# Low halves of the MLP weights on VectorE instead of GpSimd, and the first two PReLUs ahead of a decode step

## Chip, cores and metric

One core of a Trainium2 chip runs the whole kernel in one launch. The metric is device time in microseconds (us) of that core. The kernel before takes 828.43 us (median of three runs, 828.38 to 828.44). The profile is of one further execution, which took 827.54 us; the span that its records cover is 825.8 us, so 1.7 us lie around the span.

The engines are named as in the profile: PE is TensorE (PEld its weight loads), DVE is VectorE, ACT is ScalarE, POOL is GpSimd, SP is the engine that issues most of the transfers.

## What is computed

Three stages follow one another (the reference, cut):

```
attn = softmax(where(mask, q @ k.T / 8, -1e9)) @ v      # 4 x 8 heads, 576 positions, 64 wide
x    = attn as [2304, 512]
h    = x @ w_in                                          # 512 -> 2048, float64 weights
g    = max(h, 0) + alpha * min(h, 0)                     # PReLU, one alpha for each of 2048 columns
x    = g @ w_out                                         # 2048 -> 512, float64 weights
e    = argmax(x @ w_gate); out = gate * sigmoid * (relu(x @ w1[e]) @ w2[e])   # 8 experts
```

Heads 0 to 3 see a local window of 32 positions, heads 4 to 7 every 32nd position. The weights of the PReLU MLP arrive as float64 and are sent to the chip as pairs of 32-bit words.

## The kernel before

**Tiles.** The 2304 tokens are taken in six blocks of 384 (BLK). The 2048 columns of the MLP are taken in 16 chunks of 128 (NC1). For each block and each chunk there are twelve matmuls of the first product (lines 439 to 441: high times high, low times high, high times low, for four slices of the contraction), a PReLU, a split of the result into a rounded high half and a low half, and nine matmuls of the second product (lines 473 to 475).

**High and low halves.** An operand of these products is held as two tiles, the value rounded by the write to the matmul's own float type and the rest. For the weights this is done once, in the first block, by decode, chunk by chunk. One chunk is 128 partitions x 1024 values (512 of w_in, 512 of w_out). Its steps are:

- decode_a (line 402, ACT): the upper words, scaled, into a buffer called stage;
- decode_b (lines 406 and 407, DVE): a shift, and the top bits of the lower words merged in;
- decode_s (line 413, DVE): the sign merged in; after it the raw words are free;
- decode_c (line 421, ACT): the high half into the first 1024 columns of the weight tile w; and (line 422, POOL) the low half, stage minus high half, into the other 1024 columns. After line 422 the stage buffer is free. There are three such buffers.

**Order.** The order on each engine is the order in which the program issues the instructions, written out by hand. There are two parts that matter here.

The prologue is 13 attention steps (lines 1129 to 1145), in which chunk k begins its decoding at step 2 + 2k and does one step of it at each attention step, so that chunks 0 to 3 are decoded and chunk 4 has had decode_a, decode_b and decode_s when it ends. Line 1148 therefore issues nothing; line 1149 issues decode_a of chunk 5. Then, for n = 0 and 1, follow the last three matmuls of the first product, the PReLU (mlp_act) and the split (mlp_split).

The main loop (line 1170) runs over n, the pair of block and chunk. In iteration n of the first block the order is: exponentials and normalisation of one attention group, the first product of chunk n + 2, the values of an earlier group (line 328), their copy to xh on ACT (line 367) and the rest xl on DVE (line 372), the PReLU of chunk n + 2, decode_c of chunk n + 4, scores of a new group and their row maxima on DVE (line 252), decode_b and decode_s of chunk n + 5, a third of the second product of chunk n, transposes of an earlier group (line 313), the other two thirds, decode_a of chunk n + 6, and the split of chunk n + 2 (line 459 on ACT, line 460 on DVE).

Three couplings run across the engines. The first product of n + 2 writes one of two PSUM banks called h, which the split of n (line 460 last) frees. The values and the transposes share one PSUM bank T, so the transposes of an iteration wait until DVE has written xl of the same iteration (line 372). The normalisation is two small DVE instructions (lines 295 and 296) and one multiplication on POOL (line 297), which stands in POOL's queue together with line 422.

Of the kernel before, what the change touches and what calls it, by code (L numbers as in the profile page):

```python
# [7 lines left out]
F32 = mybir.dt.float32  # L8
# [3 lines left out]
AF = mybir.ActivationFunctionType  # L12
ALU = mybir.AluOpType
# [10 lines left out]
NC1 = FF // P  # L24
# [18 lines left out]
DEC = 4  # L43
# [40 lines left out]
def attention_prelu_mlp_routed_experts_kernel(  # L84
# [11 lines left out]
    nc = tc.nc  # L96
# [28 lines left out]
    with tc.manual_schedule():  # L125
# [251 lines left out]
        raw_t, w_t = {}, {}  # L377
# [6 lines left out]
        def w_tile(c, dt, name):  # L384
            return wpool.tile(
                [P, 2048], dt, tag="wa" if c < NA else "wb", name=name, bufs=NA if c < NA else NC1 - NA
            )

        def load_w(c):
            raw_t[c] = w_tile(c, I32, "raw64")  # L390
            nc.sync.dma_start(raw_t[c], wp[c].bitcast(I32))


        dec_t = {}
# [21 lines left out]
            raw_t.pop(c)  # L416

        def decode_c(c):
            t = dec_t.pop(c)
            w = w_t[c] = w_tile(c, F32R, "w")  # L420
            nc.scalar.activation(out=w[:, :1024], in_=t, func=AF.Copy)
            nc.gpsimd.tensor_tensor(out=w[:, 1024:], in0=t, in1=w[:, :1024].bitcast(F32), op=ALU.subtract)

        def w_in(c, part, k):
            return w_t[c][:, part * 1024 + k * P : part * 1024 + (k + 1) * P]
# [6 lines left out]
        def mlp_in(n, ks=range(KD)):  # L432
            blk, c = divmod(n, NC1)
            xh, xl = xt(blk)
            if n not in h_t:
                h_t[n] = bank("h", 2)
            ph = h_t[n]
            for k in ks:
                mm(ph[:, :BLK], w_in(c, 0, k), xh[:, k, :], start=(k == 0), stop=False)  # L439
                mm(ph[:, :BLK], w_in(c, 0, k), xl[:, k, :], start=False, stop=False)  # L440
                mm(ph[:, :BLK], w_in(c, 1, k), xh[:, k, :], start=False, stop=(k == KD - 1))  # L441

        def mlp_act(n):
            c = n % NC1
            ph = h_t.pop(n)
            v = ph[:, :BLK]
            a = xpool.tile([P, BLK], F32, tag="a", name="a", bufs=2)
            nc.scalar.activation(out=a, in_=v, func=AF.Relu)  # L448
            nc.scalar.activation(out=v, in_=v, func=AF.Relu, scale=-1.0)  # L449
            nc.vector.scalar_tensor_tensor(  # L450
                out=v, in0=v, scalar=nalpha[:, c : c + 1], in1=a, op0=ALU.mult, op1=ALU.add
            )
            h_t[n] = v

        def mlp_split(n):
            v = h_t.pop(n)
            gh = xpool.tile([P, BLK], F32R, tag="gh", name="gh", bufs=3)
            gl = xpool.tile([P, BLK], F32R, tag="gl", name="gl", bufs=2)
            nc.scalar.activation(out=gh, in_=v, func=AF.Copy)  # L459
            nc.vector.tensor_tensor(out=gl, in0=v, in1=gh.bitcast(F32), op=ALU.subtract)  # L460
            g_t[n] = (gh, gl)
# [606 lines left out]
        def load_ws(k):  # L1068
            for _, c in zip(range(k), loads):
                load_w(c)  # L1070
# [22 lines left out]
        def att_back(s):  # L1093
            if on(s - LV):
                att_rest(s - LV)
            for n in v_at.pop(s, ()):
                load_v(n)

        def att_step(s, tags, ttag, vtag):

            att_front(s)
            if on(s - 1):
                att_exp(s - 1)
            if on(s):
                att_scores(s, tags)
            if on(s - LV):
                att_values(s - LV, vtag)
                att_store(s - LV)
            if on(s - LT):
                att_transpose(s - LT, ttag)  # L1110
            if on(s):
                att_max(s)
            if on(s - 1):
                att_norm(s - 1)
            att_back(s)
# [4 lines left out]
        steps_done = {}  # L1120

        def decode(k, n):

            steps = [decode_a, decode_b, decode_s, decode_c]
            for f in steps[steps_done.get(k, 0) : n]:
                f(k)
            steps_done[k] = max(steps_done.get(k, 0), min(n, 4))

        for s in range(NPRO):
            att_step(s, ("h", "h") if s % 2 else ("S", "X"), "acc0" if s % 2 else "T", "acc1" if s % 2 else "acc2")  # L1130
# [4 lines left out]
            if s == 4:  # L1135
# [3 lines left out]
                    out=wg_hl[:, :, 2 * E :], in0=wg_sb, in1=wg_hl[:, :, : 2 * E].bitcast(F32), op=ALU.subtract  # L1139
                )  # L1140
                nc.vector.memset(acc_oh[:, 0, :], 0.0)
            for k in range(NC1):
                n = s - (T0[k] if k < len(T0) else 99)
                if n >= 0:
                    decode(k, n + 1)

        span[:] = [FIRST + EXTRA if EXTRA < LV else 0, NG]
        decode(DEC, 3)
        decode(DEC + 1, 1)
        for n in range(2):  # L1150
            mlp_in(n, range(KD - 1, KD))
            mlp_act(n)
            mlp_split(n)
        last = NBLK * NC1
        turn_at, logits_at = {}, {}
        for blk in range(NBLK - 1):
            for j in range(TPB):
                c = 2 * j + 1 if blk < NBLK - 2 else j
# [11 lines left out]
        for n in range(last):  # L1170
            blk, c = divmod(n, NC1)
            todo = []
            if blk + 1 < len(steps_of) and c < NC1 - 2:
                s0, s1 = steps_of[blk + 1]
                k = s1 - s0
                todo = list(range(s0 + k * c // (NC1 - 2), s0 + k * (c + 1) // (NC1 - 2)))
            for s in todo[:-1]:
                att_step(s, ("S", "X"), "T", "T")
            s = todo[-1] if todo else -9
            if on(s - 1):  # L1180
                att_exp(s - 1)
                att_norm(s - 1)
            if n + 2 < last:
                mlp_in(n + 2)
            if on(s - LV):
                att_values(s - LV, "T")
                att_store(s - LV)
            att_back(s)
            if n + 2 < last:
                mlp_act(n + 2)  # L1190
            if n + DEC < NC1:
                decode(n + DEC, 4)
            att_front(s)
            if on(s):
                att_scores(s, ("S", "X"))
                att_max(s)
            if n + DEC + 1 < NC1:
                decode(n + DEC + 1, 3)
            mlp_out(n, range(1))
            if on(s - LT):  # L1200
                att_transpose(s - LT, "T")
            mlp_out(n, range(1, 2))
            if (blk - 1, c) in logits_at:
                logits(blk - 1, logits_at[blk - 1, c])
            if (blk - 1, c) in turn_at:
                turn(blk - 1, turn_at[blk - 1, c])
            if blk > 0 and c == (7 if blk < NBLK - 1 else 4):
                gather_logits(blk - 1)
                rest = route_parts(blk - 1)
                next(rest)  # L1210
            if blk > 0 and c == (8 if blk < NBLK - 1 else 5):
                next(rest, None)
            if blk > 0 and c == (9 if blk < NBLK - 1 else 6):
                rank(blk - 1)
            mlp_out(n, range(2, TPB))
            load_ws(1)
            if n + DEC + 2 < NC1:
                decode(n + DEC + 2, 1)
            if n + 2 < last:
                mlp_split(n + 2)  # L1220
            if c == NC1 - 1 and blk == 3:
                s_a.close()
                epool = s_x.enter_context(tc.tile_pool(name="epool", bufs=1))
                idx_in = epool.tile([P, NSLOT], I32, name="idx_in")
                idx_out = epool.tile([P, NSLOT], I32, name="idx_out")
                idx_any = epool.tile([1, 1], I32, name="idx_any")
                e_i32 = epool.tile([1, NSLOT], I32, name="e_i32")
                taken = epool.tile([P, NTT], F32, name="taken")
                used = epool.tile([P, E], F32, name="used")
                nc.vector.memset(taken, 0.0)  # L1230
            if blk == NBLK - 1:
                if c == 6:
                    for _ in plan_parts(True):
                        pass
                    load_expert(0, 0)
                    load_expert(0, 1)
                if c == EL:
                    lists(True)
                    indices(True)
                if c in (9, 10, 11):  # L1240
                    gathers(0)
                if c == 11:
                    split_expert(0, 0)
                    load_expert(1, 0)
                if c == 13:
                    turn_x(0, 0)
                if c == 14:
                    turn_x(0, 1, bank("X"))
                    gathers(2)
                    split_expert(1, 0)  # L1250
                    load_expert(2, 0)
                if c == 15:
                    turn_x(1, 0)
            if c == NC1 - 1:
                evacuate(blk)
# [236 lines left out]
```

## Time and profile before

| | |
|---|---|
| median of three runs | 828.43 us |
| profiled execution / its span | 827.54 us / 825.8 us |
| PE busy | 783.3 us, 95% |
| DVE busy | 465.1 us, 56% |
| ACT busy | 427.6 us, 52% |
| POOL busy | 223.9 us, 27% |

These shares are means over stages with different limits. The page cuts the span into 40 slices of about 20.6 us; DVE reads 4979997345... in tenths, so its first 150 us are another stage than what follows. PE waits are listed by who ended them; an instruction that is itself held up while it runs shows as a long one, not as idle time, so durations of one line are compared with each other as well.

### The profile page before, as it was taken

The page shows a single profiled execution, that of the slowest core. Times are in us where ns is not written, and L with a number is a line of the kernel's source. Part 1 is how long each engine was busy: PE and PEld are TensorE (multiplying, and loading weights), DVE is VectorE, ACT ScalarE, POOL GpSimd, SP SyncE. Part 2 cuts the span into 40 slices and gives each one's busy share as a digit, 9 for nine tenths or more (in the row PEclk, how much of TensorE's full clock was granted, in tenths as well). Part 3 has the DMA queues.
Part 4 walks back from the last instruction along what each step waited for, and adds up shares of the span by engine and source line. Part 5 has one row for each costly group of instructions (what it writes and reads, how often), then busy time and mean ns, then how long its engine had stood idle before and what let it go on. Part 6 is the DMA issues. An engine that isn't in the chain of part 4 may idle for free. (4 is left out here: it accounts for less than half of the span.)

```text
span 825.8 us, 13693 instructions
## 1 busy us (share of the span) xinstructions
PE 783.3 (95%) x5035; PEld 659.0 (80%) x5035; DVE 465.1 (56%) x980; ACT 427.6 (52%) x1057; POOL 223.9 (27%) x152
## 2 busy tenths in 40 slices
PE   7778889999999999999999999999989998999996
PEld 4566767888888888888898898889879876878884
DVE  4979997345544454556333434657695447854422
ACT  6847676445544454555333333265534656655542
POOL 2734444011100011111000000113474465546422
PEclk9789899999999999999999999999999999999998
DMA  9707411111200121101000100553224577787421
GB/s 342 303 1 298 167 56 49 33 33 46 84 18 1 47 87 64 36 11 39 2 1 1 39 1 1 204 191 125 56 90 159 176 268 250 281 290 270 161 88 41
DMA packets 22621, 91.04 MB, mean 110 GB/s; under 512 B 3082, under 2 KB 7312, under 8 KB 15376
## 3 DMA queue, kind: packets, MB, share of 16 engines
q1 hardware_dynamic: 18816, 78.52, 26.8%
q0 software_dynamic: 3728, 11.55, 4.0%
q8 instruction: 41, 0.67, 0.3%
q14 instruction: 36, 0.29, 0.1%
HBM read 105.78 MB, written 9.97 MB: 140 GB/s over the span
## 5 line engine op out<-in xcount | busy, mean ns | idle before, releaser
L439 PE MATMUL h<-xh,w 128*128 128x384 f32 x384 | 131.2, 342 | 4.1 <-DVE gl L460 3.8
L440 PE MATMUL h<-xl,w 128*128 128x384 f32 x384 | 130.5, 340 | 0.7 <-DVE xl L372 0.7
L441 PE MATMUL h<-xh,w 128*128 128x384 f32 x384 | 130.4, 340 | 0.0
L450 DVE SCALAR_TENSOR_TENSOR h<-h,nalpha,a 128x384 f32<-128x384 f32 x96 | 59.9, 624 | 116.1 <-ACT h L449 116.0
L473 PE MATMUL acc<-w,gh 128*128 128x512 f32 x288 | 125.3, 435 | 0.0
L297 POOL TENSOR_TENSOR p<-p,sm 96x512 f32<-96x512 f32 (+2 forms) x47 | 48.2, 1026 | 283.6 <-DVE sm L296 260.5
L888 DVE TENSOR_TENSOR wx<-raw,wx 128x1024 fp32r<-128x1024 f32 x72 | 97.1, 1392 | 46.9 <-ACT wx L886 46.6
L475 PE MATMUL acc<-w,gl 128*128 128x512 f32 x288 | 114.3, 397 | 0.0
L474 PE MATMUL acc<-w,gh 128*128 128x512 f32 x288 | 114.1, 396 | 0.0
L448 ACT ACTIVATE a<-h 128x384 f32<-128x384 f32 x96 | 47.2, 491 | 105.9 <-PE h L441 105.9
L886 ACT ACTIVATE wx<-raw 128x1024 fp32r<-128x1024 f32 x96 | 94.6, 1056 | 7.6 <-DMA raw<-in_wexp_dram 7.6
L1042 PE MATMUL acc<-wx,hh 128*128 128x512 f32 x304 | 97.0, 401 | 0.0
L888 POOL TENSOR_TENSOR wx<-raw,wx 128x1024 fp32r<-128x1024 f32 x24 | 63.1, 2629 | 90.7 <-ACT wx L886 90.6
L439 PEld LDWEIGHTS h<-xh,w 128*128 128x128 f32 x384 | 73.4, 191 | 9.6 <-DVE gl L460 5.5
L440 PEld LDWEIGHTS h<-xl,w 128*128 128x128 f32 x384 | 73.2, 191 | 4.8 <-DVE xl L372 1.0
L441 PEld LDWEIGHTS h<-xh,w 128*128 128x128 f32 x384 | 73.2, 191 | 0.0
L460 DVE TENSOR_TENSOR gl<-h,gh 128x384 fp32r<-128x384 f32 x96 | 53.3, 555 | 33.0 <-PE acc L475 18.2
L895 POOL DMA_INDIRECT xg<-rows,idx_in x23 | 29.3, 1274 | 145.4 <-ACT h L449 139.0
L1042 PEld LDWEIGHTS acc<-wx,hh 128*128 128x128 f32 x304 | 56.6, 191 | 11.2
L475 PEld LDWEIGHTS acc<-w,gl 128*128 128x128 f32 x288 | 54.6, 190 | 13.2
L459 ACT ACTIVATE gh<-h 128x384 fp32r<-128x384 f32 x96 | 46.7, 486 | 34.8 <-DVE h L450 34.7
L473 PEld LDWEIGHTS acc<-w,gh 128*128 128x128 f32 x288 | 54.5, 189 | 10.6 <-issue 0.3
(259 smaller groups left out, 1548.3 us busy)
## 6 DMA issues: line engine op xcount, KB each, us to landing
raw<-in_wexp_dram SPq DMA_DIRECT2D x64, 1024.0 KB
raw<-in_wp_dram SPq DMA_DIRECT2D x16, 1024.0 KB
qk<-in_qkv_dram SPq DMA_DIRECT2D x10, 576.0 KB
rows<-stage SPq DMA_DIRECT2D x15, 256.5 KB
v<-in_qkv_dram SPq DMA_DIRECT2D x8, 320.0 KB
qk<-in_qkv_dram SPq DMA_DIRECT2D x4, 384.0 KB
v<-in_qkv_dram SPq DMA_DIRECT2D x6, 256.0 KB
qk<-in_qkv_dram SPq DMA_DIRECT2D x4, 224.0 KB
```

The source lines that it names most:

```text
L297: (nc.vector if gi in NRV else nc.gpsimd).tensor_tensor(out=pt[:r, :nu, :kk], in0=pt[:r, :nu, :kk], in1=sm[:r, :nu].unsqueeze(2).to_broadc ...
L439: mm(ph[:, :BLK], w_in(c, 0, k), xh[:, k, :], start=(k == 0), stop=False)
L440: mm(ph[:, :BLK], w_in(c, 0, k), xl[:, k, :], start=False, stop=False)
L441: mm(ph[:, :BLK], w_in(c, 1, k), xh[:, k, :], start=False, stop=(k == KD - 1))
L450: nc.vector.scalar_tensor_tensor(out=v, in0=v, scalar=nalpha[:, c : c + 1], in1=a, op0=ALU.mult, op1=ALU.add)
L460: nc.vector.tensor_tensor(out=gl, in0=v, in1=gh.bitcast(F32), op=ALU.subtract)
L473: mm(o, gh[:, t], w_out(c, 0), start=(c == 0), stop=False)
L474: mm(o, gh[:, t], w_out(c, 1), start=False, stop=False)
L475: mm(o, gl[:, t], w_out(c, 0), start=False, stop=(c == NC1 - 1))
L886: nc.scalar.activation(out=w[:, :1024], in_=raw, func=AF.Copy)
L888: eng.tensor_tensor(out=w[:, 1024:], in0=raw, in1=w[:, :1024].bitcast(F32), op=ALU.subtract)
L1042: mm(po[i], h[:, h0 : h0 + P], wk[:, w0 : w0 + 512], start=st, stop=sp)
```

## The change

Line 422 is taken out of decode_c and becomes a step of its own, decode_d, issued on DVE. In the prologue it comes one attention step after decode_c; in the main loop it comes after the second product of the iteration and ahead of decode_a of chunk n + 6 and the split of n + 2, that is, on DVE between line 413 and line 460. The two calls of lines 1148 and 1149 go behind the two PReLUs and splits.

```diff
         def decode_c(c):
-            t = dec_t.pop(c)
             w = w_t[c] = w_tile(c, F32R, "w")
-            nc.scalar.activation(out=w[:, :1024], in_=t, func=AF.Copy)
-            nc.gpsimd.tensor_tensor(out=w[:, 1024:], in0=t, in1=w[:, :1024].bitcast(F32), op=ALU.subtract)
+            nc.scalar.activation(out=w[:, :1024], in_=dec_t[c], func=AF.Copy)
+
+        def decode_d(c):
+            w = w_t[c]
+            nc.vector.tensor_tensor(
+                out=w[:, 1024:], in0=dec_t.pop(c), in1=w[:, :1024].bitcast(F32), op=ALU.subtract
+            )
...
-            steps = [decode_a, decode_b, decode_s, decode_c]
+            steps = [decode_a, decode_b, decode_s, decode_c, decode_d]
...
-            steps_done[k] = max(steps_done.get(k, 0), min(n, 4))
+            steps_done[k] = max(steps_done.get(k, 0), min(n, 5))
...
-        decode(DEC, 3)
-        decode(DEC + 1, 1)
         for n in range(2):
             mlp_in(n, range(KD - 1, KD))
             mlp_act(n)
             mlp_split(n)
+        decode(DEC, 3)
+        decode(DEC + 1, 1)
...
             mlp_out(n, range(2, TPB))
             load_ws(1)
+            if n + DEC < NC1:
+                decode(n + DEC, 5)
             if n + DEC + 2 < NC1:
                 decode(n + DEC + 2, 1)
```

## Rows read from the trace of the kernel before

**Rows 1.** Busy us (and instruction count) per engine, PE clock, DMA, by stretch

```profile
56.80:137.50 80.70, 69.28 (x421) 54.52 (x420) 78.31 (x112) 56.01 (x160) 36.78 (x21) 0.96 0.40 143
...
150.00:300.00 150.00, 149.91 (x933) 127.55 (x931) 72.11 (x205) 73.22 (x237) 12.21 (x13) 1.00 0.12 39
```

**Rows 2.** Waits of PE, 55 to 145 us: total, times, longest

```profile
PE T L313 <- DVE xl L372: 8.2, 7, 2.3
PE sl_bank L228 <- ACT p L281: 1.7, 3, 0.6
PE X L228 <- ACT p L281: 1.3, 3, 0.5
```

**Rows 3.** Timeline of DVE (start, length, line), two iterations

```profile
69.45 0.15 DVE L295 TENSOR_SCALAR sm<-sm 96x4 f32<-96x4 f32 x1
...
70.89 3.00 DVE L406 TENSOR_SCALAR stage<-stage 128x1024 int32<-128x1024 int32 x1
73.93 1.23 DVE L407 SCALAR_TENSOR_TENSOR stage<-raw,stage 128x1024 int32<-128x1024 int32 x1
...
78.24 0.69 DVE L406 TENSOR_SCALAR stage<-stage 128x1024 int32<-128x1024 int32 x1
78.96 3.28 DVE L407 SCALAR_TENSOR_TENSOR stage<-raw,stage 128x1024 int32<-128x1024 int32 x1
```

**Rows 4.** Timeline of POOL, the same iterations

```profile
70.98 2.35 POOL L422 TENSOR_TENSOR w<-stage,w 128x1024 fp32r<-128x1024 f32 x1
77.34 1.03 POOL L297 TENSOR_TENSOR p<-p,sm 126x504 f32<-126x504 f32 x1 [4.00 <-DVE sm L296]
78.33 2.83 POOL L422 TENSOR_TENSOR w<-stage,w 128x1024 fp32r<-128x1024 f32 x1
```

**Rows 5.** Lines of DVE, 56.8 to 137.5 us: count, busy, mean, idle

```profile
L407 DVE SCALAR_TENSOR_TENSOR stage<-raw,stage 128x1024 int32<-128x1024 int32 x11 | 21.8, 1980 | 0.4
L406 DVE TENSOR_SCALAR stage<-stage 128x1024 int32<-128x1024 int32 x11 | 21.7, 1977 | 0.0
L413 DVE SCALAR_TENSOR_TENSOR stage<-raw,stage 128x1024 int32<-128x1024 int32 x11 | 13.5, 1225 | 0.4
```

**Rows 6.** Line 888, experts' weights: ns minimum/median/maximum of one

```profile
L888 DVE TENSOR_TENSOR wx<-raw,wx x72: 1210/1220/3426, 543.8 to 807.6; 128x1024 fp32r<-128x1024 f32 x72
```

**Rows 7.** Timeline of DVE, three of them in a row

```profile
750.99 3.50 DVE L888 TENSOR_TENSOR wx<-raw,wx 128x1024 fp32r<-128x1024 f32 x3 [4.64 <-ACT wx L886]
```

**Rows 8.** Timeline of DVE, idle time in the loop

```profile
92.33 0.49 DVE L372 TENSOR_TENSOR xl<-T,xh 128x84 fp32r<-128x84 f32 x2 [1.02 <-ACT xh L367]
...
138.88 0.56 DVE L460 TENSOR_TENSOR gl<-h,gh 128x384 fp32r<-128x384 f32 x1 [1.02 <-PE acc L475]
```

**Rows 9.** Timeline of PE, two long waits

```profile
51.08 0.69 PE L439 MATMUL h<-xh,w 128*128 128x384 f32 x1 [3.69 <-DVE gl L460]
...
84.64 1.07 PE L313 MATMUL T<-cst,p 126*126 126x126 f32 x4 [2.32 <-DVE xl L372]
```

**Rows 10.** Timeline of DVE, prologue, the long ones

```profile
24.28 2.05 DVE L295 TENSOR_SCALAR sm<-sm 126x4 f32<-126x4 f32 x1
...
32.87 0.81 DVE L295 TENSOR_SCALAR sm<-sm 126x4 f32<-126x4 f32 x1 [0.78 <-ACT p L281]
...
39.43 2.33 DVE L295 TENSOR_SCALAR sm<-sm 72x2 f32<-72x2 f32 x1
...
46.20 3.18 DVE L413 SCALAR_TENSOR_TENSOR stage<-raw,stage 128x1024 int32<-128x1024 int32 x1
```

**Rows 11.** Timeline of POOL, one normalisation of the prologue

```profile
26.72 2.09 POOL L297 TENSOR_TENSOR p<-p,sm 126x504 f32<-126x504 f32 x1 [0.41 <-PE acc L328]
```

**Rows 12.** Timeline of ACT around the first two PReLUs

```profile
44.98 1.20 ACT L402 ACTIVATE stage<-raw 128x1024 f32<-128x1024 f32 x1
46.91 0.49 ACT L448 ACTIVATE a<-h 128x384 f32<-128x384 f32 x1 [0.73 <-PE h L441]
...
55.39 0.49 ACT L448 ACTIVATE a<-h 128x384 f32<-128x384 f32 x1 [3.00 <-PE h L441]
```

## The prediction

> **What bounds the kernel now.** I read the busy times by stretch first, because the change touches only the first 150 us. From 150 to 300 us PE is busy 149.91 of 150 us: there PE is the bound, and whatever is won or lost earlier is handed on as it stands. From 56.8 to 137.5 us it is another stage: PE is busy 69.28 of 80.70 us, DVE 78.31 [rows 1]. PE leaves 11.4 us idle, DVE 2.4. The waits of PE say which engine it waits for: 8.2 us of the transposes for xl from DVE, 3.0 us of the scores for exponentials on ACT [rows 2].
>
> Next, whether DVE has that much to do. In the timeline of DVE line 406 takes 3.00 us at 70.89 and 0.69 us at 78.24, with the same tile; line 407 takes 1.23 us at 73.93 and 3.28 us at 78.96 [rows 3]. The POOL timeline shows what differs: line 422 runs from 70.98 to 73.33 and from 78.33 to 81.16 [rows 4]. The long DVE instruction ends, both times, about its own short length after POOL's end (73.89 is 0.56 after 73.33; 82.24 is 1.08 after 81.16). So a DVE instruction that meets line 422 does not run slower, it stands still until POOL is done. DVE's full bar is in part time in which DVE is held.
>
> How much: in the loop the eleven of line 406, of 407 and of 413 sum to 21.7 + 21.8 + 13.5 = 57.0 us [rows 5]. Free of POOL they take 0.69, 1.23 and 1.22 us, 11 x 3.14 = 34.5 us (line 413's mean is its free length). The held time is 22.5 us, 2.05 us for each chunk.
>
> **The change, part by part.**
>
> *Line 422 leaves POOL, in the loop.* The 22.5 us go, if nothing else on POOL holds those lines. What is left there is line 297, 1.03 us, begun right behind the normalisation's second DVE instruction [rows 4]; at 78.24 line 406 starts 0.13 us before it ends and still takes 0.69 us, so 0 to 0.1 us each, left out.
>
> *Line 422's work comes to DVE, in the loop.* No such instruction stands there now. The nearest is line 888: same operation, same tile, same types: 1.21 us at the least, 1.22 at the median, 3.43 at the most [rows 6]; three in a row take 3.50 us [rows 7], which is (3.50 - 1.22) / 2 = 1.14 us apart. I take 1.17 us, between 1.14 and 1.22. The 3.43 us is one that met a POOL instruction; here POOL has none at that place, line 297 being done four instructions earlier, so it is the outer end only. Of the twelve in the loop, eleven lie on the path of DVE: 11 x 1.17 = 12.9 us (12.5 to 13.4). The twelfth, of chunk 15, falls where DVE already idles 1.02 us for PE [rows 8]; without that cover it would cost 1.17.
>
> Net on DVE: 22.5 - 12.9 = 9.6 us (9.1 to 10.0), an iteration going from 7.35 us (70.89 to 78.24) to 6.5. Is it the path? PE can give back at most its 11.4 us of idle time, more only by a higher clock, so 9.6 fits under PE's bound, but closely: PE has (80.70 - 11.4) / 11 = 6.3 us of work in an iteration. PE is late next, with some 0.2 us of waiting per iteration left.
>
> *A wait that is added.* The weights of a chunk are complete only when DVE has written the low half, and the first product of n + 2 then waits for DVE instead of POOL. It cannot be the last wait: the low half of n + 2 is written in iteration n - 2 (it is the fourth step ahead), just before line 460 of chunk n, and the same product waits for that line 460 as well, to get its PSUM bank. What is queued behind the new instruction on DVE is line 460, the normalisation, xl and the PReLU, and PE's transposes and products wait for these; that is the 1.17 us per iteration already charged.
>
> *Stage buffers.* They come free by DVE instead of POOL, in the iteration before the one whose decode_a takes them. I cost this at nothing: line 421 stands between on ACT. If that cover went, ACT would wait at most 1.17 us in an iteration, and its busy time, 56.01 of 80.70 us [rows 1], leaves 2.2 us for it.
>
> *The prologue.* Four of line 422 hold DVE there: line 295 for 2.05, 0.81 and 2.33 us, against 0.15 for the same line when free [rows 3], and line 413 for 3.18 against 1.22 [rows 10, 5]: 1.9 + 0.66 + 2.18 + 1.96 = 6.7 us. Four new instructions cost 4 x 1.17 = 4.7. Net 2.0 us. Following the order of the instructions by hand from 24 us on, with the short lengths, the first PReLU's DVE instruction comes 2.1 us earlier, and the product that starts 3.69 us late at 51.08, waiting for line 460 [rows 9], starts as much earlier. Bounds: if each new instruction keeps a POOL normalisation waiting for its whole length and that is passed on, 2.0 - 4.7 = -2.7 us; if only the held time counts and the new instructions fall into gaps, +6.7. I take 2.0, as DVE is nearly full there too.
>
> One rule bears on this. The normalisation at 26.72 took 2.09 us instead of 1.03, while line 413 ran [rows 11, 4]: POOL stands still for DVE as well. The Trainium skill, "SBUF — State Buffer", section "Who interferes with whom", has it that a DVE instruction with two SBUF inputs and a GpSimd instruction that reads SBUF exclude each other, and that the one which issues first keeps the other out for its whole length. The rows agree in both directions. By that rule the new DVE instruction, which has two SBUF inputs, can itself hold the normalisation, up to 1.22 us each time; in the loop it comes long after it, in the prologue it may not. That is the lower bound above, and a rival below.
>
> *The PReLUs go ahead.* Of the two calls moved only one issues anything: one ACT instruction, line 402 at 44.98. Behind it ACT idled 0.73 us for PE before the PReLU, so it was not in the way; in its new place it falls into the 3.00 us before 55.39 [rows 12]. Nothing is moved on DVE, PE or the transfer queue. Cost 0 (gain at most the 0.47 us by which its 1.20 would exceed that gap; loss 0).
>
> **Sum.** 2.0 + 9.6 = 11.6 us from the profiled 827.54 us: 815.9. The median lies 0.89 us above the profiled execution: 816.8 us. Own range of this case: 9.1 to 10.0 for the loop and, from the inner part of the prologue's bounds, 0.5 to 4 give 9.6 to 14.0 us, 814.4 to 818.8.
>
> **Rivals.**
>
> *A. PE takes over and stays partly at its low clock: smaller gain.* PE has one wait of 2.32 us at 84.64 [rows 9], and the granted clock of the loop is 0.96 of the upper level [rows 1]. If the new, closer schedule still has that wait and the low clock behind it, if DVE's idle 1.02 us behind it [rows 8] remains, or if the normalisations of the prologue are held by the new instruction, the gain is 4 to 9 us: 819 to 824. For it: PE's margin is only 0.2 us an iteration. Against: PE keeps less idle time in any case.
>
> *B. Larger gain.* If the shorter waits keep PE at the full clock from 47 us on and the prologue's normalisations no longer stand behind line 422 in POOL's queue, 3 to 5 us more: 812 to 814. For it: 24 to 29 us shows a normalisation kept by both. Against: DVE sets the pace, not PE.
>
> *C. Slower: DVE is full and gets more work.* If the long instructions are long for a reason other than line 422 (their overlap with POOL being only a matter of the order), nothing goes and 11 x 1.22 + 4 x 1.22 = 18 us come on top of a full DVE: 846 us. It turns slower as soon as the held time that goes is under 1.2 us per chunk, instead of 2.05. For it: DVE has only 2.4 us of idle time. Against: held lines change with POOL's timing, sometimes 406 and sometimes 407.
>
> *D. No change.* The time won is given back before the end, for instance at the transition to the experts. Against: PE is full for hundreds of us in between, so everything moves as a block. 828.
>
> **Chances.** Forecast 0.60, A 0.20, B 0.11, C 0.06, D 0.03. A change within 0.2% (1.7 us) is what a measurement of this kernel can't tell from none. Faster 0.91, same 0.03, slower 0.06. The range 812.3 to 822.5 leaves out C, D, the far end of A and a little of B, some 0.15.
>
> **What would show it.** Lines 406 and 407 without lengths near 3 us; twelve low halves on DVE in the loop at 1.14 to 1.25 us; the DVE iteration at 6.4 to 6.6 us; the waits of PE for xl below 4 us instead of 8.2; the product at 51.08 about 2 us earlier, and all that follows 150 us moved by one constant amount. The prediction is wrong if lines 406 and 407 stay long, if the low halves take 2 us or more, or if PE's idle time stays at 11 us under another name.

## The result and the profile after

The changed kernel takes 815.38 us (median of four runs, 814.98 to 817.40); the ratio to the kernel before is 0.9839, 95% interval 0.9811 to 0.9866, so 13.3 us faster (11.1 to 15.7) against 11.6 predicted. The medians differ by 13.0 us; the ratio counts a fourth run of the kernel before as well, of 831.42 us. The profiled execution took 817.40 us, the longest of the four, with a span of 815.6 us. In what follows the 16 low halves are line 424 on DVE, and the lines below it have moved by four or more (450 is 454, 460 is 464, 497 is 501).

Busy time by stretch, columns as in [rows 1]. The first is the same eleven iterations of the loop as 56.8 to 137.5 us before:

```profile
55.30:125.20 69.90, 66.85 (x421) 53.65 (x420) 68.38 (x123) 55.74 (x160) 8.94 (x10) 0.98 0.45 163
...
150.00:300.00 150.00, 149.91 (x953) 126.77 (x952) 73.90 (x213) 74.20 (x246) 14.28 (x15) 1.00 0.13 45
```

The stretch is 80.70 - 69.90 = 10.8 us shorter. PE does the same 421 matmuls; its idle time falls from 11.4 to 3.05 us. DVE is still full: 68.38 of 69.90 us. The stage behind it is as full of PE as it was.

The lines of DVE in that stretch, to be held against [rows 5]:

```profile
L407 DVE SCALAR_TENSOR_TENSOR stage<-raw,stage 128x1024 int32<-128x1024 int32 x11 | 13.5, 1226 | 0.4
L413 DVE SCALAR_TENSOR_TENSOR stage<-raw,stage 128x1024 int32<-128x1024 int32 x11 | 13.5, 1225 | 0.4
L424 DVE TENSOR_TENSOR w<-stage,w 128x1024 fp32r<-128x1024 f32 x11 | 13.4, 1217 | 0.0
L406 DVE TENSOR_SCALAR stage<-stage 128x1024 int32<-128x1024 int32 x11 | 7.6, 690 | 0.0
```

Lines 407 and 406 fall from 1980 and 1977 ns to 1226 and 690. With 413 the three sum to 34.6 us instead of 57.0: 22.4 us of held time are gone. Line 424 comes with 1217 ns each.

The waits of PE around the loop, 53.5 to 133 us, beside [rows 2]:

```profile
PE T L313 <- DVE xl L372: 1.4, 3, 0.6
PE sl_bank L228 <- ACT p L281: 1.3, 1, 1.3
PE X L228 <- ACT p L281: 0.4, 1, 0.4
```

One iteration on DVE, the one that answers to 78.24 in [rows 3] (the columns are start, length, line):

```profile
80.22 0.68 DVE L406 TENSOR_SCALAR stage<-stage 128x1024 int32<-128x1024 int32 x1
80.94 1.23 DVE L407 SCALAR_TENSOR_TENSOR stage<-raw,stage 128x1024 int32<-128x1024 int32 x1
82.20 1.23 DVE L413 SCALAR_TENSOR_TENSOR stage<-raw,stage 128x1024 int32<-128x1024 int32 x1
83.34 1.22 DVE L424 TENSOR_TENSOR w<-stage,w 128x1024 fp32r<-128x1024 f32 x1
84.48 0.55 DVE L464 TENSOR_TENSOR gl<-h,gh 128x384 fp32r<-128x384 f32 x1
...
86.80 0.68 DVE L406 TENSOR_SCALAR stage<-stage 128x1024 int32<-128x1024 int32 x1
```

Nothing stands still, and line 406 comes again after 6.58 us; in the mean of the eleven an iteration takes 69.90 / 11 = 6.35 us, instead of 7.34. Line 424 begins 1.14 us before line 464: its 1.22 us overlap the next by 0.08.

**How the win travels.** The transposes behind the first block are a marker that every kernel has (the row gives ns minimum/median/maximum, then the first and last start in us). The first row is the kernel before, the second the changed one:

```profile
L497 PE MATMUL T<-cst,stage x60: 270/273/332, 169.0 to 501.9; 128*128 128x128 f32 x60
```

```profile
L501 PE MATMUL T<-cst,stage x60: 270/273/332, 156.7 to 489.5; 128*128 128x128 f32 x60
```

12.3 us at the first, 12.4 at the last: it goes through the PE-bound blocks as a block. Of these 12.3 us, 1.5 lie ahead of the loop (its stretch starts at 55.30 instead of 56.80) and 10.8 in it. Among the experts this execution lost some: POOL's instruction at 690.62 before is at 678.39 after (12.2 earlier), the next at 700.13 is at 689.60 (10.5 earlier). On POOL, before and after:

```profile
690.62 1.80 POOL L895 DMA_INDIRECT xg<-rows,idx_in  x1
700.13 2.87 POOL L888 TENSOR_TENSOR wx<-raw,wx 128x1024 fp32r<-128x1024 f32 x1 [7.70 <-ACT wx L886]
```

```profile
678.39 1.80 POOL L899 DMA_INDIRECT xg<-rows,idx_in  x1 [0.16 <-issue]
689.60 2.48 POOL L892 TENSOR_TENSOR wx<-raw,wx 128x1024 fp32r<-128x1024 f32 x1 [9.41 <-ACT wx L890]
```

Between them ACT waited 1.59 us for a load of expert weights, which it did not do at that place before. The three runs without a profile are 1.7 to 2.4 us shorter than the profiled one; whether they had this wait is not known.

### The profile page after: what moved, and what is told of

Read it like the earlier page. It is cut to its first block, busy times and chain, and to the rows that moved or that the text cites. A ratio compares the mean times of both kernels' runs of the same rounds, so it can differ in the third digit from the quotient of the medians.

```text
span 815.6 us, 13687 instructions
## 1 busy us (share of the span) xinstructions
PE 781.1 (96%) x5032; PEld 658.1 (81%) x5035; DVE 454.5 (56%) x996; ACT 427.4 (52%) x1057; POOL 180.9 (22%) x136
## 4 chain that ended last, share of the span: by engine, by line
PE 76%; DVE 8%; issue 3%; ACT 2%; DMA 1%; POOL 0%; SPq 0%; ACTq 0%; DVEq 0%; POOLq 0%
PE acc L1046 10%; PE acc L477 8%; PE acc L479 7%; PE acc L478 7%; PE h L443 7%; PE h L445 7%; PE h L444 7%; PE sl_bank L234 2%; PE T L328 2%; DVE wx L892 2%; PE T L313 2%; PE h L969 1%; PE h L971 1%; PE h L970 1%; PE sl_bank L910 1%
## 5 line engine op out<-in xcount | busy, mean ns | idle before, releaser
L297 POOL TENSOR_TENSOR p<-p,sm 96x512 f32<-96x512 f32 (+2 forms) x47 | 48.2, 1025 | 333.4 <-DVE sm L296 283.0
L890 ACT ACTIVATE wx<-raw 128x1024 fp32r<-128x1024 f32 x96 | 94.7, 1055 | 12.2 <-DMA raw<-in_wexp_dram 12.2
```

The lines of the kernel that those rows point to most:

```text
L297: (nc.vector if gi in NRV else nc.gpsimd).tensor_tensor(out=pt[:r, :nu, :kk], in0=pt[:r, :nu, :kk], in1=sm[:r, :nu].unsqueeze(2).to_broadc ...
L890: nc.scalar.activation(out=w[:, :1024], in_=raw, func=AF.Copy)
```

## The experiments

Totals vary by up to 5 us among the runs of one kernel; so each is read by its ratio to the kernel before on the same chip and, from its profile, by the marker (169.0 before, 156.7 after). The marker comes from one execution each. How far that can be trusted shows in three kernels whose code is the same but for one ACT instruction up to the first PReLU: they reach it on DVE at 48.82 us (the loop alone), 49.30 (before) and 49.83 (the move alone). Differences of the marker of 1 us or less are therefore not read as an effect.

**Only the move.**

```diff
-        decode(DEC, 3)
-        decode(DEC + 1, 1)
         for n in range(2):
             ...
+        decode(DEC, 3)
+        decode(DEC + 1, 1)
```

> The kernel before (828.4 us) with only the two PReLUs moved ahead of the decode calls; the low halves stay on GpSimd. My theory (the call moved issues one ACT instruction into idle time): 828.4, between 827.6 and 829.2. Rival (part of the gain of the change comes from the PReLUs being earlier): 827 or less, and the first line 450 on VectorE at 48.2 us instead of 49.3.

Ratio 0.9999 (0.9987 to 1.0012), marker 169.5. The move does nothing that a total resolves (about 1 us either way), and the first line 450 comes at 49.83 us, not at the rival's 48.2. ACT in this kernel shows why:

```profile
47.42 0.49 ACT L448 ACTIVATE a<-h 128x384 f32<-128x384 f32 x1 [1.81 <-PE h L441]
...
52.81 1.14 ACT L402 ACTIVATE stage<-raw 128x1024 f32<-128x1024 f32 x1
55.91 0.49 ACT L448 ACTIVATE a<-h 128x384 f32<-128x384 f32 x1 [1.97 <-PE h L441]
```

Line 402 has gone from in front of one wait of ACT for PE, which grew from 0.73 to 1.81 us, into another, which shrank from 3.00 us [rows 12] to 1.97 us.

**Only the engine.** The changed kernel with those lines put back.

> The changed kernel (815.4 us) without the move of the PReLUs. My theory: 815.4, between 814.5 and 817.5. Rival: it lies 1 us or more above the changed kernel because line 402 of the sixth chunk stands ahead of the first PReLU on ACT, 816.5 to 818.5 with the first line 454 later than 48.6 us.

Ratio 0.9845 (0.9817 to 0.9872), marker 155.9: the whole gain without the move. The first PReLU's DVE instruction came at 47.5 us, not later than 48.6.

**Loop only, prologue only.** (`c >= NA` in the second)

```diff
         def decode_c(c):
             ...
+            if c < NA:
+                nc.gpsimd.tensor_tensor(
+                    out=w[:, 1024:], in0=dec_t.pop(c), in1=w[:, :1024].bitcast(F32), op=ALU.subtract
+                )
         def decode_d(c):
+            if c < NA:
+                return
```

> The changed kernel, but chunks 0 to 3 get their low halves on GpSimd, right behind the high halves, as before. My theory: the loop's share of the gain alone, 828.4 - 10.8 = 817.6, between 816.3 and 818.6. Rival (the loop wins only because the prologue leaves it a better start, with PE at its upper clock): above 820.

> The changed kernel, but chunks 4 to 15 get their low halves on GpSimd as before. My theory: the prologue's share alone, 828.4 - 1.5 = 826.9, between 825.5 and 827.8, and the two shares (this and the loop alone) add up to the whole 13 us within 1 us. Rival (a better start is worth more in the loop): 824 or less.

The loop alone: 0.9873 (0.9845 to 0.9901), 10.5 us; the prologue alone: 0.9979 (0.9967 to 0.9990), 1.7 us. The markers, loop alone and then prologue alone:

```profile
L507 PE MATMUL T<-cst,stage x60: 270/273/332, 158.7 to 491.5; 128*128 128x128 f32 x60
```

```profile
L507 PE MATMUL T<-cst,stage x60: 270/273/331, 166.6 to 499.4; 128*128 128x128 f32 x60
```

10.3 and 2.4 us, 12.7 together, beside 12.3 with both and 13.1 with both and no move. Within that spread the shares add up, and neither needs the other. By the ratios both lie in the ranges expected of them.

**The new place, the old engine.**

```diff
         def decode_d(c):
             w = w_t[c]
-            nc.vector.tensor_tensor(
+            nc.gpsimd.tensor_tensor(
```

> The changed kernel with its decode_d step at the new place, but issued on GpSimd. My theory (the engine matters, not the place): within 2 us of 828.4, with lines 406 and 407 at 3 us as often as before. Rival (the later place gives the gain): 815 to 820, on whatever engine.

Ratio 1.0014 (1.0000 to 1.0029), marker 168.8. Its DVE lines from 57 to 138 us:

```profile
L407 DVE SCALAR_TENSOR_TENSOR stage<-raw,stage 128x1024 int32<-128x1024 int32 x11 | 21.8, 1980 | 0.4
L406 DVE TENSOR_SCALAR stage<-stage 128x1024 int32<-128x1024 int32 x11 | 21.7, 1976 | 0.0
```

They are the lines of before to the nanosecond or two. It is the engine, not the place.

**Twice on GpSimd.**

```diff
-            nc.gpsimd.tensor_tensor(out=w[:, 1024:], in0=t, ...)
+            for _ in range(2):
+                nc.gpsimd.tensor_tensor(out=w[:, 1024:], in0=t, ...)
```

> The kernel before with line 422 issued twice in a row on GpSimd (the second writes the same values). My theory (VectorE stands still while it runs): 2.0 to 2.3 us more held time for each of 15 chunks on the path, 855 to 865 us, and a second of lines 406, 407 and 413 near 3 us in each iteration. Rival (the long instructions are long for another reason, and GpSimd, busy 27%, has room): 828 to 831 us.

856.72 us, ratio 1.0333 (1.0295 to 1.0371), 27.6 us more. On DVE, and then on POOL, in one iteration:

```profile
80.68 3.00 DVE L406 TENSOR_SCALAR stage<-stage 128x1024 int32<-128x1024 int32 x1
83.72 3.28 DVE L407 SCALAR_TENSOR_TENSOR stage<-raw,stage 128x1024 int32<-128x1024 int32 x1
87.04 1.22 DVE L413 SCALAR_TENSOR_TENSOR stage<-raw,stage 128x1024 int32<-128x1024 int32 x1
```

```profile
80.77 5.15 POOL L423 TENSOR_TENSOR w<-stage,w 128x1024 fp32r<-128x1024 f32 x2
```

Two instructions on POOL, two held on DVE; the third, which starts after POOL's end at 85.92, is short. So it is in the whole loop: line 407 takes 3296 ns in the mean, and 406 and 413, of which one is held in each iteration, 1893 and 2056. With the experiment before it this settles rival C: the long instructions are long because of line 422.

**Twice on VectorE.**

```diff
         def decode_d(c):
             w = w_t[c]
+            t = dec_t.pop(c)
+            for _ in range(2):
                 nc.vector.tensor_tensor(... in0=t, ...)
```

> The changed kernel with the low half computed twice in a row on VectorE. My theory (VectorE still sets the pace): 15 x 1.14 = 17 us more, less the 1 to 3 us that PE waits now anyway, 828 to 832 us. Rival (PE sets the pace after the change, VectorE has room): at most 5 us more, below 820.

837.46 us, ratio 1.0094 (1.0060 to 1.0129), marker 175.8, 19.1 us behind the changed kernel. The expectation was low. The pair took, with the line behind it:

```profile
62.89 2.48 DVE L426 TENSOR_TENSOR w<-stage,w 128x1024 fp32r<-128x1024 f32 x2
65.28 0.55 DVE L466 TENSOR_TENSOR gl<-h,gh 128x384 fp32r<-128x384 f32 x1
```

2.39 us to the next line's start instead of 1.14: the second instance costs 1.25, not 1.14, perhaps because it writes the tile that the first is writing (not tested). 15 x 1.25 = 18.8 us is close to the marker's 19.1: DVE's added work was not hidden, and PE waits for xl again:

```profile
PE T L313 <- DVE xl L372: 12.1, 7, 3.5
```

The total grew by 22.1 us; the 3 us beyond the marker's are within the spread of the runs (834.6 to 838.1).

**No low halves.**

```diff
         def decode_d(c):
-            w = w_t[c]
-            nc.vector.tensor_tensor(...)
+            dec_t.pop(c)
         def w_in(c, part, k):
-            return w_t[c][:, part * 1024 + k * P : part * 1024 + (k + 1) * P]
+            return w_t[c][:, k * P : (k + 1) * P]
         def w_out(c, part):
-            return w_t[c][:, part * 1024 + 512 : part * 1024 + 1024]
+            return w_t[c][:, 512:1024]
```

> The changed kernel without the low halves of the MLP's weights on any engine; PE multiplies by the high half a second time in their place, so its work is the same. My theory (PE is next, with 3.05 us idle from 54 to 125 us, and the prologue gives some more): 808 to 812 us. Rival (VectorE alone sets the pace): 15 x 1.14 = 17 us less, 798 us.

808.71 us, ratio 0.9747 (0.9720 to 0.9775), marker 151.3: of the 17 us by which DVE is relieved only 5.4 arrive by the marker, 6.7 by the medians and 7.6 by the ratios. Its busy times from 53 to 120 us:

```profile
53.00:120.00 67.00, 65.57 (x419) 53.94 (x418) 57.08 (x110) 54.41 (x159) 9.10 (x10) 0.97 0.47 168
```

PE is busy 65.57 of 67.00 us and DVE has 9.9 us to spare: PE has taken over. Even of the 5.4 us, 3.3 are, in these two executions, won ahead of the loop (the third PReLU on DVE comes at 51.51 us instead of 54.79); the loop itself gives 2.1 us, less than the 3.05 us that PE idled there. So the changed kernel stands where the two bounds are close: more work on DVE costs at full price, less of it gains little in the loop.

**Normalisations of the prologue on VectorE.** An attempt at a better version, since POOL's multiplication (line 297) and DVE still hold each other in the prologue.

```diff
-NRV = (9,)
+NRV = (8, 9)            # e9;  e10: (4, 5, 7, 8, 9)
```

> The changed kernel with the multiplication of the normalisation of attention group 8 (line 297, held by line 406 and holding line 407 in the prologue) on VectorE instead of GpSimd. My theory (each engine stands still for the other): VectorE gains 0.7 us of held time for 0.6 us of work, and PE's wait of 1.58 us for it shrinks, so the end of the first block comes 0 to 1.5 us earlier: 814 to 816 us. Rival (VectorE is full, any work on it costs): 816 to 817 us.

> The changed kernel with the multiplications of groups 4, 5, 7, 8 and 9 of the prologue on VectorE. My theory: four holds of 0.7 to 0.85 us go, some 2.5 to 3 us of work come, so VectorE is even, and PE's four waits for GpSimd's normalisations (4.8 us together) shrink by half: 812 to 815.5 us. Rival (VectorE is full, any work on it costs): 817 to 818 us.

Ratios 0.9847 (0.9820 to 0.9874) and 0.9859 (0.9831 to 0.9886), markers 155.1 and 155.9. Beside 156.7 and 155.9 of the changed kernel with and without the move this is 0 to 1.6 us earlier, and in the total there is nothing that can be told from the changed kernel. The hold does go; in the first of the two, line 407 is short where it was 1.93 us long:

```profile
36.43 0.68 DVE L297 TENSOR_TENSOR p<-p,sm 126x504 f32<-126x504 f32 x1
37.03 0.29 DVE L372 TENSOR_TENSOR xl<-acc,xh 128x48 fp32r<-128x48 f32 x2
37.24 0.69 DVE L406 TENSOR_SCALAR stage<-stage 128x1024 int32<-128x1024 int32 x1
37.96 1.23 DVE L407 SCALAR_TENSOR_TENSOR stage<-raw,stage 128x1024 int32<-128x1024 int32 x1
```

but line 297 takes 0.68 us on DVE for the 0.70 that it frees. By its ratio the first (815.8 us) is at the upper end of what I expected; the second (816.7 us) is beyond it: PE's waits for the normalisations ahead of 55 us fell from 5.2 to 2.4 us, but brought nothing that can be seen by the end of the block. Neither is a better version.

## Why the prediction was right

- *DVE is the bound of the loop, and part of its full bar is standing still.* Shown: with the engine put back at the new place the long lines are back, with GpSimd's work doubled there are twice as many.
- *Line 422 leaves: 22.5 us.* Measured 57.0 - 34.6 = 22.4.
- *The new work: 11 x 1.17 = 12.9 us.* Measured 1217 ns each, 1.14 us apart from the next line: 12.5 us of DVE's time, the lower end of what I gave. The nearest row, another line of the same shape [rows 6, 7], gave it.
- *Net 9.6 us in the loop.* This was 1.2 too low, and the 10.8 lie outside my own 9.1 to 10.0. DVE's busy time fell by 78.31 - 68.38 = 9.9 us, and its idle time from 2.4 to 1.5: the wait of 1.02 us behind PE's long stall [rows 8] went with the stall. I had left that idle time as it was in the sum. 9.9 + 0.9 = 10.8. An iteration therefore takes 6.35 us in the mean, a little under the 6.4 to 6.6 that I had named as the sign.
- *PE late next, by a small margin.* Shown from both sides: a second low half on DVE costs its whole 19 us, taking the low half away gives 5 to 8 of 17.
- *The added wait cannot be last.* No wait of any engine for line 424 appears in the profile, so the stage buffers cost nothing either.
- *The prologue: 2.0 us.* With the prologue alone the marker says 2.4 and the ratio 1.7 (0.8 to 2.7); in the changed kernel the loop's stretch starts 1.5 earlier. The first PReLU on DVE comes at 48.21 instead of 49.30, and the product of 51.08, which I expected about 2 us earlier, at 49.99: 1.1 us earlier each. One execution says little here. The three kernels with the old prologue reach that PReLU at 48.82, 49.30 and 49.83, the three with the new one and no other change (after, without the move, prologue alone) at 48.21, 47.51 and 48.04; the means differ by 1.4 us, under the 2.1 that I followed by hand. One thing that I left out of the sum, and allowed for only in the lower bound, is in the trace: a mutual hold. The first row is DVE before, the other three are DVE after; POOL after follows:

```profile
34.20 1.98 DVE L413 SCALAR_TENSOR_TENSOR stage<-raw,stage 128x1024 int32<-128x1024 int32 x1
```

```profile
25.50 1.21 DVE L424 TENSOR_TENSOR w<-stage,w 128x1024 fp32r<-128x1024 f32 x1
26.63 2.05 DVE L413 SCALAR_TENSOR_TENSOR stage<-raw,stage 128x1024 int32<-128x1024 int32 x1
...
33.26 1.97 DVE L424 TENSOR_TENSOR w<-stage,w 128x1024 fp32r<-128x1024 f32 x1
```

```profile
25.51 2.09 POOL L297 TENSOR_TENSOR p<-p,sm 126x504 f32<-126x504 f32 x1 [2.45 <-DVE sm L296]
```

At 25.50 DVE began the first line 424; POOL's normalisation, 10 ns later, took 2.09 us instead of 1.03, and line 413 behind it then stood still for 0.8 us (2.05 instead of 1.22). That hold is new. The second line 424 stood still for a normalisation too, but before, line 413 did so at 34.20: that hold has only passed from one line to another. A new hold of 0.8 us is of the size of what is missing; that it is all of it is not shown. So each engine kept the other out here, in both directions, but the prologue stayed far above the lower bound of -2.7 us. Which of the two goes first can't always be read from the listed starts: at 70.89 line 406 is listed 0.09 us ahead of line 422, and it was line 406 that stood still [rows 3, 4].

- *The PReLUs: 0.* Two kernels show no cost and no gain, to about 1 us.
- *Rival A (PE at its low clock).* The granted clock of the loop rose from 0.96 to 0.98, and the wait of 2.32 us before the transposes is gone; the longest is 0.6. Between 47 and 57.5 us the clock was 0.67 before and 0.84 after, but the kernel without the move shows 0.67 there and the total of the changed one, and the kernel with GpSimd at the new place 0.84 and the total of before, so the gain doesn't hang on it.
- *Rival B (larger gain).* The interval of the ratio alone (11.1 to 15.7 us) reaches into it. Its conditions did not come: the clock from 47 to 57.5 us was 0.84 and not full, and the prologue gave about the 2 us of the forecast, not 3 to 5 more.
- *Rival D (given back).* Not in the blocks behind, which move by 12.3 us throughout; 2 us were lost among the experts in the profiled execution, so there the shift was not constant as I had said.
- *The sum: 11.6 us.* By the marker it is 12.3, 1.5 + 10.8 against my 2.0 + 9.6. The mechanism is the one that I described, but that the sum came so close is in part luck: the loop's term was 1.2 too small and the prologue's, in this execution, 0.5 too large.

## What to carry over

A full bar of an engine is not a full load of it: compare the durations of one line with each other, and where they fall into a short and a long kind, look for what runs on the other engine in the long ones. Work that is put on the fullest engine can make it faster, if the same work held it for longer from elsewhere (here 2.05 us held for 1.14 us of work). Then look at once for the next bound: here a further relief of DVE by 17 us was worth 5 to 8 us, and in the loop, where PE was next, only 2.

Not every instruction of DVE is held. In the kernel before, line 252 reads PSUM, and two of it kept their 0.42 us inside line 422 on POOL; line 295, behind them, reads and writes SBUF and was held, 0.81 us instead of 0.15 [rows 10]. DVE and then POOL:

```profile
31.35 0.42 DVE L252 TENSOR_REDUCE nm<-sl_bank 126x2 f32<-126x252 f32 x1
31.68 0.42 DVE L252 TENSOR_REDUCE nm<-X 126x2 f32<-126x252 f32 x1
```

```profile
31.16 2.50 POOL L422 TENSOR_TENSOR w<-stage,w 128x1024 fp32r<-128x1024 f32 x1 [1.54 <-ACT w L421]
```

So it matters which work of one engine is laid beside which work of the other.

## What was not expected

- Two low halves in a row on the same tile cost 2.39 us, 2 x 1.14 + 0.11, where three of another line on different tiles were 1.14 us apart [rows 7].
- With line 422 on POOL twice in a row (5.15 us), DVE got one instruction in between: POOL's pair took 5.15 us for two of about 2.35, and DVE's two held instructions followed each other at 80.68 and 83.72. The first ended at 83.68, 0.56 us after the 83.12 at which a first POOL instruction of 2.35 us would have ended, the second at 87.00, 1.08 us after the pair's end: the same 0.56 and 1.08 us as with one POOL instruction. So here the engines took turns, instruction by instruction, as far as the ends tell; the two POOL instructions stand in one row.
- Runs of the kernel before on one chip differ by up to 5 us. Where two profiles could be laid beside each other, 2 us were lost among the experts, in a stage that the change does not touch.
